# TensorE visits the attention once for two chunks from chunk 12 on; correction words in place; half of the down weights converted directly

## The chip, the cores and the metric

One core of one Trainium2 chip. The metric is the device time of one execution in microseconds (us). The kernel before was run three times.

## The reference, cut to what matters

Two stages. The first is a causal linear attention with a decay per head over (4, 8, 768, 64), in blocks of 64 tokens; the second takes its output as 3072 tokens of 512 values through a leaky ReLU layer pair. All inputs are 64-bit or 32-bit floats from the host's arrays; the weights (512x2048 and 2048x512) come as 64-bit floats.

```
for b in range(nb):
    intra = einsum('bhic,bhjc->bhij', qb, kb) * Dmask
    intra = einsum('bhij,bhjd->bhid', intra, vb)
    inter = einsum('bhid,bhde->bhie', qb * lam_pow, kv_state)
    out[:, :, sl] = intra + inter
    kv_state = lam_block * kv_state + einsum('bhsd,bhse->bhde', kb * rev_pow, vb)
x = out.transpose(0, 2, 1, 3).reshape(B * S, H * D)
h = x @ w_in
return maximum(0.01 * h, h) @ w_out
```

## The kernel before, in words

**Chunks and groups.** The 3072 tokens are 24 chunks of 128 (six to a batch), and four chunks make a group: six groups of 512 tokens. The attention works chunk by chunk, the layer pair group by group.

**Attention (L410, L546, L637 to L718).** For each chunk: load k, q and v; bring k and q into transposed form (on TensorE with `transpose`, L546, for chunks 0 to 9; for later ones by many small loads of 32x32 blocks, L509, and StreamTransposes on DVE, L518); scores into the PSUM tile psc (16 matmuls of 64x64) and state products k'v (16 matmuls, into the upper half of psc from chunk 4 on); on DVE the masking with the decay (L637, into the tile sc) and the state additions (L644); on POOL the decay of the state (L647), the scaling of k (L585) and of q (L592). The output of the chunk goes to the PSUM tile po: `own` (16 matmuls) and `inter` in two halves (8 and 8). The second half waits for a small read of po by DVE or ACT (L676). On TensorE a stay in the attention is: outputs of chunk c up to the first half of inter, then state products and scores of chunk c + 1, then the second half of inter of c: 64 matmuls, which the trace shows as two records each. These stays are called visits below.

**Splits.** A 32-bit value is carried to TensorE as three fp32r parts, high, low and mixed (h, l, m). Chunk outputs are split by ACT (L692, xh), DVE (L700, xl; L718, xm) into X of their group (two sets). The weights are split in `parts` (L807 or L809 wh, L812 wm, L814 wl) into W[p], p = 0 to 7, which the up weights fill first and the down weights later.

**64-bit weights.** `to_float32` (L764) makes 32-bit floats of a half row block: a load into one of the three buffers raw; on ACT, L793 (the upper words to w32), L795 and L797 (16-bit correction words, written to a dense buffer low0 or low1); on DVE a shift (L799) and the addition of the correction (L800).

**Up products (L850).** For each group g and weight block p: 2 halves x 3 parts x 4 = 24 matmuls of 512 columns into two of four PSUM banks (pt, b10, b11, b2); ACT applies the leaky ReLU (L877) into one of two tiles gs, and a DMA writes it to DRAM (L880). These and the down products are called wide matmuls below: 1152 and 1152.

**Down weights.** `w_out` converts one half of a row block at a time during groups 2 and 3 and writes it as 32-bit floats to DRAM (L829); in the last group `w_out_parts` (L831) reads a row block back and splits it into W[p] once the up product with W[p] is done.

**Down products (L916).** `down_load` (L888) reads a pair (g, p) back into one of four buffers over the attention's memory, splits it (L897 ACT, L898 and L900 DVE) into one of four ring slots, which lie over X; `down` accumulates pairs of p into eight PSUM accumulators.

**Order.** Every operation is entered into `Plan` with the tiles it reads and writes. The list ORDER (L266) gives operation numbers and engines in the order in which they stand in the program; what it doesn't name, `emit` places by the listed costs. Engines run their own operations in that order. SP issues all loads and stores but two. Negative entries of ORDER are fill matmuls on the identity (`busy`, L349) on TensorE.

Of the kernel before, what the change touches and what calls it, by code (L numbers as in the profile page):

```python
# [44 lines left out]
class Plan:  # L45
# [8 lines left out]
    def __init__(self, kinds, also, member):  # L54
        self.ops, self.rank = [], 0.0
        self.chain, self.chains = None, {}
        self.warm, self.slack, self.more = 0.0, 0.0, {}
        self.first = {"PE": 0.0, "ACT": 0.0, "DVE": 3.4, "POOL": 0.0, "DMA": 0.2}
        self.cold, self.idle, self.order = 4.75, None, []
        self.kinds, self.also, self.member = kinds, also, member  # L60
        self.deps, self.keys = None, None
# [24 lines left out]
    def resolve(self, program):  # L86

        last = {}
        ended = {x: -1 for names in self.kinds.values() for x in names}
        holds = dict.fromkeys(ended)  # L90
# [149 lines left out]
def kernel(  # L240
# [26 lines left out]
    APART = 4  # L267
    FIRST_LOADS = ["k0", "q0", "v0", "k1", "q1", "v1", "w10", "k2", "q2", "v2", "w11", "k3", "q3", "v3"]
    LOW_PE, MIX_PE = set(), set()
    PAIRS = {"q": set()}  # L270
    QS = 8
    KM = 8
    NRAW = 3
    TURN = 3
    SLACK, GSLACK = 4.0, 2.0
    EARLY_SLACK = 1.0
    GOFIRST = 3
    SUBL, FIRST = 0.75, -8.0

    DV = 10  # L280
    RUNS = {10: (-8.0, 0.8), 12: (4.0, 0.0)}
# [24 lines left out]
    raw = [sb([P, 2 * d_model], f"raw{i}") for i in range(NRAW)]  # L306
    lows = [sb([P, d_model], f"low{i}", I32) for i in range(2)]
    w32 = sb([P, 2, d_model], "w32")
    w32f = w32.rearrange("p h n -> p (h n)")
    tt = [raw[-1][:, i * T:(i + 1) * T] for i in range(2)]  # L310
    gs = [sb([P, 2, T], f"gs{i}") for i in range(2)]
    WO = [dram.tile([P, 2 * d_model], F32, name=f"wo{p}", tag=f"wo{p}") for p in range(NP)]
    G = [[dram.tile([P, 2 * T], F32, name=f"g{g}_{p}", tag=f"g{g}_{p}") for p in range(NP)] for g in range(NG)]


    NA = 9120
    att = sb([P, NA], "att")
# [24 lines left out]
    make_identity(nc, ident)  # L342

    def busy(n, at):

        wide = bank[at].rearrange("p (a t) -> p a t", t=C2)
        for i in range(0, n, 8):
            k = min(8, n - i)
            nc.tensor.matmul(wide[:, :k, :], lhsT=ident, rhs=_bc(ident[:, 0:C2], 1, k), start=True, stop=True, skip_group_check=True)  # L349

    busy(WARM, "b2")
    nc.gpsimd.memset(zero, 0.0)
    LATE_W = 5
    neg_i, pos_s = [W[LATE_W][2][:, i * P:(i + 1) * P] for i in range(2)]
    kinds = {"bank": list(bank), "raw": [f"raw{i}" for i in range(NRAW)], "low": ["low0", "low1"], "gs": ["gs0", "gs1"]}
    also = {"gs0": ["gs00", "gs01", "k@2", "v@2"], "gs1": ["gs10", "gs11", "k@3", "v@3"], f"raw{NRAW - 1}": [f"raw{NRAW - 1}", "q@3"], "psc": ["psc0", "psc1"], "po": ["po0", "po1"]}
    early = [Slot("gs", 0), Slot("gs", 1), Slot("raw", NRAW - 1)]
    plan = Plan(kinds, also, {"k@2": early[0], "v@2": early[0], "k@3": early[1], "v@3": early[1], "q@3": early[2]})
# [73 lines left out]
    def spot(nm, c):  # L432

        if (nm, c) in spots:
            return spots[nm, c].rearrange("p (h d) -> p h d", h=H), f"{nm}@{c}"
        return kqv["kqv".index(nm)][c % 2], f"{nm}{c % 2}"
# [33 lines left out]
    def run(c):  # L470

        lo = max(DV, c - c % TURN)
        return lo, c - c % TURN + TURN - lo
# [8 lines left out]
    def subs(first, n):  # L482


        n = n * C
        def rows(x, lo, hi):
            return x[:, :(hi - lo) * n].rearrange("p (y t) -> p y t", t=n), lo, hi
        ks = [(*rows(raw[-2], 0, 2), [hold(first, f"raw{NRAW - 2}")]), (*rows(raw[-1], 2, 4), [hold(first, f"raw{NRAW - 1}")])]
        qs = [(*rows(kqv_f[1], 0, HP), ["q0", "q1"])]

        if first == DV:
            ks = [(*rows(raw[0], 0, HP), [hold(first, "raw0")])]
        elif first < DV + TURN:
            qs = [(*rows(w32f, 0, 2), ["w320", "w321"])] + [
# [243 lines left out]
    def round_of(c):  # L738

        after = []  # L740
        if c + 2 < NCH:
            load_kq(c + 2)
# [8 lines left out]
        for x in after:  # L751
            x()
# [288 lines left out]
```

## Time and profile before

| | |
|---|---|
| three runs, us | 606.93, 608.06, 608.13 (median 608.06) |
| the profiled execution | 607.55 us, span 605.8 us, granted TensorE clock 0.999 |
| loads and stores | 105.18 MB in 147753 packets, 123632 of them under 512 bytes |
| DMA queue of SP | 59.2% of 16 engines' span |
| TensorE idle before its matmuls from 41 to 126 us | none; 0.48 us at 126.8 us |
| up products end, down products begin | about 341 us |

A trace row of TensorE is one record; PE is the matmul side, PEld the weight loads that run beside it. A group's mean lasts from its issue to its modelled end, so rows that overlap sum to more than the time they take; how far groups start from each other tells what they cost. DVE is VectorE, ACT ScalarE, POOL GpSimd, SP SyncE.

### The profile page before, as it was taken

The numbers are of one execution on the slowest core, as the hardware profiler recorded it, in microseconds if no ns is written. First come the engines' busy times: TensorE is split into PE (matmuls) and PEld (weight loads), VectorE is DVE, ScalarE is ACT, GpSimd is POOL, SyncE is SP. The second block draws the span as 40 slices with busy tenths as digits, with TensorE's granted clock in tenths as the row PEclk, the third lists the DMA queues.
The fourth block names the chain that finished last, engine by engine and source line by source line (L and its number), as shares of the span: only waits on it lengthen the run. The fifth ranks groups of instructions, "written<-read, shape, count | busy, mean of one in ns | idle before, by whom it ended". The sixth has DMA issues, their size and how long they took to land.

```text
span 605.8 us, 12704 instructions
## 1 busy us (share of the span) xinstructions
PE 597.7 (99%) x5376; PEld 494.6 (82%) x5376; DVE 296.5 (49%) x403; ACT 213.3 (35%) x329; POOL 79.2 (13%) x85
## 2 busy tenths in 40 slices
PE   8899999999999999999999999999999999999997
PEld 6788888878888888888888888888888888888886
DVE  6899865351453343244466764354353443534430
ACT  3677562212433343342555431222312313214111
POOL 2432532133132031033000000000000000000000
PEclk9999999999999999999999999999999999999999
DMA  9999877677888887774696842524333333333201
GB/s 208 246 255 270 222 194 193 124 190 186 236 198 219 233 234 202 192 227 160 204 349 245 291 160 84 160 85 139 124 109 135 111 132 122 123 104 123 86 1 69
DMA packets 147753, 105.18 MB, mean 174 GB/s; under 512 B 123632, under 2 KB 124400, under 8 KB 147696
## 3 DMA queue, kind: packets, MB, share of 16 engines
q1 hardware_dynamic: 147408, 104.29, 59.2%
q8 instruction: 42, 0.69, 0.5%
q14 instruction: 15, 0.12, 0.1%
q10 hardware_dynamic: 288, 0.07, 0.1%
HBM read 68.69 MB, written 35.65 MB: 172 GB/s over the span
## 4 chain that ended last, share of the span: by engine, by line
PE 96%; DVE 3%; issue 0%; POOL 0%; DVEq 0%; POOLq 0%
PE b L850 34%; PE b L916 16%; PE psc L916 11%; PE po L916 11%; PE pt L850 10%; PE pt L916 5%; PE po L410 4%; PE psc L410 3%; PE b L349 1%; PE po L546 0%; PE b L546 0%; DVE att L637 0%; DVE w L800 0%; PE pt L546 0%; DVE att L592 0%
## 5 line engine op out<-in xcount | busy, mean ns | idle before, releaser
L898 DVE SCALAR_TENSOR_TENSOR xl<-att,xh 128x1024 fp32r<-128x1024 f32 x48 | 58.7, 1223 | 126.4 <-ACT xh L897 126.4
L897 ACT ACTIVATE xh<-att 128x1024 fp32r<-128x1024 f32 x48 | 50.7, 1060 | 146.9 <-PE pt L916 69.9
L850 PE MATMUL b<-xl,wl 128*128 128x512 f32 (+1 forms) x304 | 79.9, 389 | 0.3 <-DVE wl L814 0.3
L850 PE MATMUL b<-xh,wh 128*128 128x512 f32 (+1 forms) x304 | 79.5, 391 | 0.0
L877 ACT ACTIVATE gs<-b 128x512 f32<-128x512 f32 x75 | 44.0, 596 | 98.9 <-PE b L850 77.0
L850 PE MATMUL b<-xm,wm 128*128 128x512 f32 (+1 forms) x304 | 78.3, 389 | 0.0
L850 PEld LDWEIGHTS b<-xl,wl 128*128 128x128 f32 x304 | 56.3, 188 | 12.4 <-DVE wl L814 0.4
L850 PEld LDWEIGHTS b<-xm,wm 128*128 128x128 f32 x304 | 56.2, 188 | 11.7
L850 PEld LDWEIGHTS b<-xh,wh 128*128 128x128 f32 x304 | 55.9, 188 | 11.6
L900 DVE SCALAR_TENSOR_TENSOR xm<-xl,xh 128x1024 fp32r<-128x1024 f32 x48 | 58.8, 1226 | 4.8
L916 PE MATMUL b<-wl,xl 128*128 128x512 f32 x144 | 56.0, 389 | 0.0
L916 PE MATMUL b<-wh,xh 128*128 128x512 f32 x144 | 56.0, 389 | 0.0
L916 PE MATMUL b<-wm,xm 128*128 128x512 f32 x144 | 56.0, 389 | 0.0
L647 POOL TENSOR_TENSOR att<-att 128x256 f32<-128x256 f32 x40 | 32.8, 819 | 106.4 <-DVE att L644 92.8
L916 PE MATMUL psc<-wm,xm 128*128 128x512 f32 (+1 forms) x100 | 38.2, 387 | 0.0
L916 PE MATMUL po<-wm,xm 128*128 128x512 f32 (+1 forms) x100 | 37.9, 384 | 0.0
L916 PE MATMUL po<-wh,xh 128*128 128x512 f32 x96 | 37.3, 389 | 0.0
L916 PE MATMUL psc<-wl,xl 128*128 128x512 f32 x96 | 37.3, 389 | 0.0
L916 PE MATMUL po<-wl,xl 128*128 128x512 f32 x96 | 37.3, 389 | 0.0
L916 PE MATMUL psc<-wh,xh 128*128 128x512 f32 x96 | 37.3, 389 | 0.0
L410 PEld LDWEIGHTS po<-att 64*64 64x64 f32 x1408 | 26.7, 134 | 8.1 <-issue 6.5
L410 PE MATMUL po<-att 64*64 64x64 f32 x1408 | 32.5, 222 | 0.5 <-DVE att L676 0.3
(105 smaller groups left out, 861.6 us busy)
## 6 DMA issues: line engine op xcount, KB each, us to landing
att<-g SPq DMA_DIRECT2D x48, 512.0 KB, 3.4
g<-gs SPq DMA_DIRECT2D x47, 512.0 KB, 3.6
raw<-in_moe_w_in_dram SPq DMA_DIRECT2D x16, 512.0 KB, 4.9
raw<-in_moe_w_out_dram SPq DMA_DIRECT2D x16, 512.0 KB, 4.4
out_dram<-gs SPq DMA_DIRECT2D x23, 256.0 KB, 2.2
att<-in_k_dram SPq DMA_DIRECT2D x44, 128.0 KB, 3.5
att<-in_v_dram SPq DMA_DIRECT2D x22, 256.0 KB, 4.2
wo<-w SPq DMA_DIRECT2D x8, 512.0 KB, 4.0
```

The lines of the kernel that those rows point to most:

```text
L349: nc.tensor.matmul(wide[:, :k, :], lhsT=ident, rhs=_bc(ident[:, 0:C2], 1, k), start=True, stop=True, skip_group_check=True)
L410: nc.tensor.matmul(dst[HALF[cols]], lhsT=lhsT[HALF[rows]], rhs=rhs[HALF[rows]], start=start, stop=True, skip_group_check=True)
L647: add("POOL", 0.62, lambda new=new, j=j: nc.gpsimd.tensor_tensor(state[(j + 1) % 4], new, _bc(lam_c, 2, D), op=ALU.mult), [f"st{j % 4}", " ...
L850: nc.tensor.matmul(dst, lhsT=w[z][:, kk * 2 * P + f * P:kk * 2 * P + (f + 1) * P], rhs=x[z][:, kk, toks], start=start and kk == 0, stop=kk ...
L877: add("ACT", ns, lambda b=b, r=r: nc.scalar.activation(out=r(), in_=b(), func=AF.Prelu, bias=0.0, scale=1.0, alpha=0.01), [kb], [kg], rank ...
L897: add("ACT", 1.05, lambda: nc.scalar.activation(out=h, in_=graw[j], func=AF.Copy, bias=0.0, scale=NEAR), reads, wr("h"))
L898: add("DVE", 1.215, lambda: nc.vector.scalar_tensor_tensor(l, graw[j], 1.0, h.bitcast(F32), op0=ALU.mult, op1=ALU.subtract), reads + [f"rh ...
L900: add("DVE", 1.215, lambda: nc.vector.scalar_tensor_tensor(m, l.bitcast(F32), -S, h.bitcast(F32), op0=ALU.mult, op1=ALU.add), [f"rh{j}", f ...
L916: nc.tensor.matmul(to[:, cols], lhsT=ring[j][z][:, f * T + tb * P:f * T + (tb + 1) * P], rhs=W[pp][z][:, f * d_model:(f + 1) * d_model][:, ...
```

## The change

Three edits, and a new ORDER list for all of it.

1. **Pairs.** From chunk 12 on the attention advances by two chunks. `pair_of(c)` enters `outputs([c, c + 1])`: own of both, first halves of inter of both, one small read of po, the scores and state products of c + 2 and c + 3, second halves of both. Odd chunks use the upper halves of psc and po, which state products and transposes had; state products of a pair go to two of the four banks of the up products, the even chunk in the lower half of both, the odd one in the upper. The masked scores of odd chunks (L665, two operations of 256 columns) lie in the ends of raw1 and raw2; v of every other pair in raw3; a fifth state buffer in the end of w32. The one visit behind chunk 11 already holds the scores of 12 and 13.
2. **Correction words in place.** The two buffers low go and a fourth raw comes. ACT writes the 16-bit correction words into the lower 32-bit word of each 64-bit one in raw (L870, L872), and DVE adds that word, every second one of raw, to w32 (L875). raw is held until that addition is done.
3. **Down weights.** p = 0 to 3 go through DRAM as before, a half at a time at a slower pace; p = 4 to 7 are loaded, converted and split in the last group (`w_out_direct`), without the way through DRAM.

The fill matmuls, loads and operations of the first 118 us stand in another order in the new list. The diff, cut:

```diff
-    NRAW = 3
+    NRAW = 4
-    DV = 10
+    DV, DW, M0 = 10, 12, 12
+    PHASE, SPREAD, NVIA = 2, 24, 4
-    lows = [sb([P, d_model], f"low{i}", I32) for i in range(2)]
+    state.append(w32f[:, 3 * HP * D:].rearrange("p (y d) -> p y d", y=HP))
+    sc_odd = [raw[1 + x][:, 3 * HP * D:].rearrange("p (y t) -> p y t", y=HP) for x in range(2)]
+    v_more = [raw[3][:, i * H * D:(i + 1) * H * D].rearrange("p (h d) -> p h d", h=H) for i in range(2)]
...
+    def banks_of(c):
+        return shared.setdefault(c // 2, [Slot("bank") for _ in range(2)])
...
-        apart = c < APART
-        kp = [Slot("bank") for _ in range(n_pu)] if apart else ["psc"] * n_pu
+        apart, odd = c < APART or c >= M0, c >= M0 and c % 2 == 1
+        kp = (banks_of(c) if c >= M0 else [Slot("bank") for _ in range(2)])[:n_pu] if apart else ["psc"] * n_pu
+        cols = slice(T // 2, T) if odd else slice(0, T // 2)
...
+            if odd:
+                for x in range(2):
+                    add("DVE", 0.42, lambda x=x: nc.vector.tensor_tensor(sc_odd[x], psc[:, x, upper, :], decay[:, x], op=ALU.mult), [psck, "fk"], [("sca", "scb")[x]])
...
+        for c, at, pok, needs, inter in todo:
+            add("PE", 0.235, lambda inter=inter: inter(0), needs + ["begun"], [pok], kind="q")
+        add(("DVE", "ACT"), (0.15, 0.25), lambda e: (nc.vector.tensor_copy if e == "DVE" else nc.scalar.copy)(seen_po, po[:, :, at.start, 0]),
+            [x[2] for x in todo], ["seen_po"], rank=-3.0)
         between()
+        for c, at, pok, needs, inter in todo:
+            add("PE", 0.235, lambda inter=inter: inter(1), needs + ["seen_po", "begun"], [pok], kind="q")
...
+    def pair_of(c):
+        after = []
+        plan.begin(c)
+        more = [x for x in (c + 2, c + 3) if x < NCH]
+        after.insert(0, outputs([c, c + 1], lambda: after.extend(scores(x) for x in more)))
+        plan.end()
+        for x in after:
+            x()
+        for x in more:
+            transposes(x)("s")
+        for x in (c + 4, c + 5):
+            if x < NCH:
+                follow(x)
...
         def addend(dt, i):
-            return low().bitcast(dt).rearrange("p (n two) -> p n two", two=2)[:, :, i]
+            return r().bitcast(dt).rearrange("p (n four) -> p n four", four=4)[:, :, i]
...
-        add("DVE", 0.69, lambda: nc.vector.tensor_tensor(d, d, low(), op=ALU.add), [kl], [key], lock=True)
+        add("DVE", 0.69, lambda: nc.vector.tensor_tensor(d, d, words(0, I32), op=ALU.add), [kr], [key], lock=True)
...
+        to_float32("wo", p, h, w32[:, 0, :], "w320", after)
+        move(0.8, lambda: nc.sync.dma_start(out=WO[p][:, h * d_model:(h + 1) * d_model], in_=w32[:, 0, :]), ["w320"], [f"WO{p}"])
+
+    def w_out_direct(p):
+        for h in range(2):
+            to_float32("wo", p, h, w32[:, h, :], f"w32{h}", (), h)
+        parts(p, w32f, ["w320", "w321"])
...
-        if nxt < NCH and nxt // GC < g + 2 and n % 2 == 0:
-            seq.append(("r", nxt))
-            nxt += 1
-        if n_out < 2 * NP and n >= 1:
+        if nxt < NCH and nxt // GC < g + 2 and n % 4 == PHASE:
+            seq.append(("p", nxt))
+            nxt += 2
+        if n_out < 2 * NVIA and n * 16 >= SPREAD * n_out + 16:
...
-            w_out_parts(x[1])
+            (w_out_parts if x[1] < NVIA else w_out_direct)(x[1])
```

More of the change, by code (lines that the diff above doesn't have):

```diff
@@ L487, in rows @@
             return x[:, :(hi - lo) * n].rearrange("p (y t) -> p y t", t=n), lo, hi
-        ks = [(*rows(raw[-2], 0, 2), [hold(first, f"raw{NRAW - 2}")]), (*rows(raw[-1], 2, 4), [hold(first, f"raw{NRAW - 1}")])]
+        ks = [(*rows(raw[1], 0, 2), ["kr1"]), (*rows(raw[2], 2, 4), ["kr2"])]
         qs = [(*rows(kqv_f[1], 0, HP), ["q0", "q1"])]
[L491 to L494, printed above, removed]
-                (*rows(lows[i].bitcast(F32), 2 + i, 3 + i), [hold(first, f"low{i}")]) for i in range(2)]
+        if first < DW:
+            ks = [(*rows(raw[3], 0, HP), [hold(first, "raw3")])]
+        elif first == DW:
+            qs = [(*rows(raw[0], 0, 2), [hold(first, "raw0")]), (*rows(w32f, 2, 4), ["w320", "w321"])]
         return ks, qs
@@ L630, in scores @@
         if c < GOFIRST:
-            add("PE", 0.47, go, [f"kT{i}", f"qT{i}"], ["psc"], kind="q")
+            add("PE", 0.47, go, [f"kT{i}", f"qT{i}"], [psck], kind="q")
         add("PE", 0.47, kv, [kk, kv_], kp, kind="q")
         if c >= GOFIRST:
-            add("PE", 0.47, go, [f"kT{i}", f"qT{i}"], ["psc"], kind="q")
+            add("PE", 0.47, go, [f"kT{i}", f"qT{i}"], [psck], kind="q")
         def uses():
-            add("DVE", 0.685, lambda: nc.vector.tensor_tensor(sc, psc[:, :, lower, :], decay, op=ALU.mult), ["psc", "fk"], ["sc"])
+            while waiting and not odd:
+                waiting.pop()()
@@ L638, in uses @@
+            if odd:
+                for x in range(2):
+                    add("DVE", 0.42, lambda x=x: nc.vector.tensor_tensor(sc_odd[x], psc[:, x, upper, :], decay[:, x], op=ALU.mult), [psck, "fk"], [("sca", "scb")[x]])
+            else:
+                add("DVE", 0.685, lambda: nc.vector.tensor_tensor(sc, psc[:, :, lower, :], decay, op=ALU.mult), [psck, "fk"], ["sc"])
             for t in range(n_pu):
                 j = 2 * c + t
-                new = state[j % 4]
+                at_j = turn_of(j)
+                new = state[at_j]
@@ L721, in outputs, with less @@
-        return uses
+        add("ACT", 0.595, lambda: nc.scalar.activation(out=tok(xh), in_=y, func=AF.Copy, bias=0.0, scale=NEAR), [pok], [h])
+        if c in LOW_PE:
+            def less():
+                for t in range(2):
+                    nc.tensor.matmul(y[:, t], lhsT=neg_i, rhs=tok(xh)[:, t], start=False, stop=True, skip_group_check=True)
+            add("PE", 0.26, less, [h, "neg_i", f"wm{LATE_W}"], [pok])
+            add(("ACT", "DVE"), (0.6, 0.685), lambda e: copy(e, tok(xl), y), [pok], [l])
+        else:
+            add("DVE", 0.685, lambda: nc.vector.tensor_tensor(tok(xl), y, tok(xh.bitcast(F32)), op=ALU.subtract),
+                [pok, h], [l])
@@ new lines, in split, with mix, negate @@
+        if c in MIX_PE:
+            mk = Slot("bank")
+            z = lambda: bank[mk.name].rearrange("p (k t) -> p k t", k=KO)
+            def mix():
+                nc.tensor.matmul(z(), lhsT=neg_i, rhs=xh, start=True, stop=False, skip_group_check=True)
+                nc.tensor.matmul(z(), lhsT=pos_s, rhs=xl, start=False, stop=True, skip_group_check=True)
+            add("PE", 0.46, mix, [h, l, "neg_i", "pos_s", f"wm{LATE_W}"], [mk])
+            def negate(e):
+                if e == "ACT":
+                    nc.scalar.activation(out=xm, in_=z(), func=AF.Copy, bias=0.0, scale=-1.0)
+                else:
+                    nc.vector.tensor_scalar(xm, z(), -1.0, None, op0=ALU.mult)
+            add(("ACT", "DVE"), (0.6, 0.685), negate, [mk], [m], rank=LATER if c < GC else 0.0)
+        else:
+            add("DVE", 0.69, lambda: nc.vector.scalar_tensor_tensor(xm, xl.bitcast(F32), -S, xh.bitcast(F32), op0=ALU.mult, op1=ALU.add),
+                [h, l], [m], rank=LATER if c < GC else 0.0, lock=True)
@@ L740, in round_of @@
         after = []
-        if c + 2 < NCH:
+        if c + 2 < NCH and c != M0 - 1:
             load_kq(c + 2)
@@ L1001 @@
                 add("DVE", 0.0, lambda: None, [], ATT + [f"gr{j}" for j in range(NR)])
-                add("ACT", 0.0, lambda: None, [], [f"raw{j}" for j in range(NRAW)] + ["t0", "t1"])
+                add("ACT", 0.0, lambda: None, [], ["raw0", "sca", "scb", "kr1", "kr2", "v2", "v3", "t0", "t1"])
+                add("DVE", 0.0, lambda: None, [], ["w320", "w321", "st4"])
                 freed = True
-            w_out_parts(x[1])
+            (w_out_parts if x[1] < NVIA else w_out_direct)(x[1])
         elif x[0] == "dl":
```

202 lines of the change are left out of this document (106 added, 96 removed), and 2 rows, old and new, of the table seq.

## The prediction

> **What bounds the kernel now.** First the page's busy shares, then the same by stretches (columns: microseconds; PE, PEld, DVE, ACT and POOL busy with their instructions; clock; DMA share; GB/s).
>
> ```profile
> PE 597.7 (99%) x5376; PEld 494.6 (82%) x5376; DVE 296.5 (49%) x403; ACT 213.3 (35%) x329; POOL 79.2 (13%) x85
> ```
>
> ```profile
> 9.00:29.00 20.00, 17.13 (x478) 14.23 (x470) 17.57 (x33) 12.87 (x22) 8.56 (x9) 1.00 1.00 247
> 29.00:57.00 28.00, 27.94 (x553) 24.20 (x553) 26.81 (x41) 20.61 (x37) 9.41 (x9) 1.00 1.01 263
> 57.00:118.00 61.00, 61.00 (x625) 50.23 (x624) 36.72 (x54) 28.15 (x49) 18.76 (x16) 1.00 0.74 188
> 118.00:295.00 177.00, 176.52 (x2292) 145.94 (x2291) 68.70 (x135) 62.40 (x114) 40.69 (x44) 1.00 0.75 207
> 295.00:341.00 46.00, 46.00 (x204) 38.04 (x203) 28.66 (x30) 23.32 (x35) 0.00 (x0) 1.00 0.78 279
> 341.00:606.00 265.00, 261.48 (x1157) 216.65 (x1155) 113.83 (x96) 63.52 (x72) 0.00 (x0) 1.00 0.35 114
> ```
>
> From 57 us on TensorE never starves; only TensorE's own time can be saved there. Before that, DVE is as full as TensorE (26.81 of 28 us), and between 9 and 29 us it is ahead of it: the chain of waits runs through DVE almost without a break from 12.8 to 26.9 us.
>
> What TensorE's time consists of, from the chain and from TensorE's timeline (start, length, group):
>
> ```profile
> 327.56 8.16 PE b L850 x36
> ```
>
> ```profile
> 163.19 0.93 PE L410 MATMUL po<-att 64*64 64x64 f32 x48
> 163.94 1.11 PE L410 MATMUL psc<-att 64*64 64x64 f32 x64
> 164.87 0.41 PE L410 MATMUL po<-att 64*64 64x64 f32 x16
> 165.21 1.19 PE L850 MATMUL b<-xm,wm 128*128 128x512 f32 x4
> 166.25 1.08 PE L850 MATMUL b<-xh,wh 128*128 128x512 f32 x4
> ```
>
> ```profile
> 292.21 0.93 PE L410 MATMUL po<-att 64*64 64x64 f32 x48
> 293.07 1.19 PE L850 MATMUL b<-xh,wh 128*128 128x512 f32 x4
> 294.20 0.46 PE L410 MATMUL po<-att 64*64 64x64 f32 x16
> ```
>
> A wide matmul takes 8.16 / 36 = 0.2267 us; the 2304 of them are 522.3 us of the 605.8 us span and don't change. A visit to the attention has 128 records and lasts from 163.19 to 165.21, 2.02 us. The wide runs between such visits last 0.23 us longer than their count times 0.2267 (0.13 at the head: 165.21 to 166.25 is 1.04 us for four that need 0.91; the rest at the tail). So a visit costs 2.25 us. The short one at 292.21 has 48 records and costs 0.86 + 0.22 = 1.08. Two equations: (2.25 - 1.08) / 80 = 14.6 ns a record, and **0.38 us for the visit itself**.
>
> **The change, part by part.** All sums start from the profiled execution, 607.55 us (span 605.8, 1.75 around it); the three runs have a median of 608.06.
>
> *Pairs.* I counted both instruction orders on TensorE: 1472 attention matmuls, 80 transposes and 2304 wide ones in each, so nothing is removed but visits. Behind the 308th wide matmul the order before has 15 visits, the new one 10 (one pair is cut in two, the last in two). 5 x 0.38 = **-1.9 us**. What could hide or undo it: the waits inside a visit. The second half of the state products waits for the small read of po (L676, 0.155 us), which the scores of two chunks (about 1.9 us) now cover instead of one. A pair's state products hold two of the four banks until four additions (0.41 each) and three decays on POOL (0.82 each) are done, some 5 us with their handovers; the up products then have two banks, 2.72 us each, against an eviction of 0.60. If ACT is late there, each pair loses up to 0.6 us (6 pairs: 3.6 us); I take 0, since 2.1 us cover it. xh, xl and xm of the second chunk come one split later (0.59 + 0.68 + 0.79 us); the nearest use is 24 wide matmuls (5.4 us) behind its visit.
>
> *Loads.* DVE and SP meet the pair at its first visit, behind wide matmul 340, which wants the transposed k and q of chunks 12 and 13; before, only chunk 12 was wanted, 8 wide matmuls earlier, and it was late:
>
> ```profile
> 127.26 1.16 PE L410 MATMUL psc<-att 64*64 64x64 f32 x64 [0.48 <-issue]
> ```
>
> Up to the last of the small loads of that run SP now issues 149 DMAs instead of 153 (0.47 us each), 1.9 us earlier, and the visit comes 8 wide matmuls (1.8 us) later. Against that stand four more StreamTransposes of 0.43. I leave the 0.5 us as it is: 0, with a bound of 2.6 us above (1.7 for the transposes and a landing of 2.8, less SP's 1.9).
>
> *The new written-out order in the first 57 us.* TensorE's fill matmuls (L349) sum to 5.63 rows of 512 columns before and 4.75 now; a row takes 0.893 us:
>
> ```profile
> L349 PE MATMUL b<-att 128*128 128x512 f32 x4 | 3.2, 893 | 1.4 <-POOL att L352 1.4
> ```
>
> They stand in for waits, so 0.88 x 0.89 = **-0.8 us**, if the waits are what the order supposes. On DVE, four operations that stood ahead of the second xm (L585 0.68, L637 0.68, L644 0.41, L700 0.68: 2.45 us) stand behind it now. Only L585 is gone (to POOL, 1.19); the rest is owed later, while DVE is still full, so I take no more than the 0.8.
>
> *Correction words in place.* ACT's three operations keep their count. The addition on DVE (L800) now reads every second 32-bit word of raw instead of a dense buffer. The rows:
>
> ```profile
> L800 DVE CUSTOM_DVE_ANT_0 w<-w,low 128x1024 uint16<-128x1024 uint16 x32 | 24.1, 764 | 6.4 <-ACT low L797 5.0
> L793 ACT ACTIVATE w<-raw 128x512 f32<-128x512 f32 x32 | 21.2, 667 | 6.9 <-DVE wm L812 3.5 <-DMA raw<-in_moe_w_in_dram 2.1 <-DMA raw<-in_moe_w_out_dram 1.3
> L898 DVE SCALAR_TENSOR_TENSOR xl<-att,xh 128x1024 fp32r<-128x1024 f32 x48 | 58.7, 1223 | 126.4 <-ACT xh L897 126.4
> ```
>
> No row shows DVE on such words. A gain is excluded: the same 512 additions. ACT reads just these words in 0.667 us where a dense 512 takes 0.59, +0.08; a DVE pass over as many words as the stride spans (L898) takes 0.46 more than L800. Between 0 and +0.46 I take +0.2, nearer to ACT's row, which reads the very same words. Ten of the 32 lie before 63.4 us, where the parts of the fifth weight are done and DVE is full: 2.0 us. Part of it lands in slack: wl of the last four of these weights is done 0.9 to 1.9 us before TensorE takes it (63.41 against 64.3 for the last), 1.2 us for the last two. So **+0.8 us** (0 to 3.4).
>
> [...]
>
> *Down weights.* Four of eight are no longer converted early, written out and read back; eight halves (ACT 0.667 + 0.788 + 0.782, DVE 0.574 + 0.764 each) move behind 295 us, where TensorE has no gap to give. Tightest is the mixed part (xm) of the sixth split of group 0, p = 5. Counted from the last up matmul: DVE does four ring splits (4.9 us), the rest of weight 6 (4.1) and a half of weight 7 (1.3), which fills the 48 wide matmuls (10.9 us) until ring slots come free; then ACT 1.06, splits and weight 7 on DVE 10.6: 22.6 us. It is wanted 104 wide matmuls on, at 23.6. Cost **0**; three strided additions at +0.2 still fit, at +0.46 it is 0.4 us late, once. The cover is thin.
>
> **Sum:** 607.55 - 1.9 - 0.8 + 0.8 = 605.65, and 0.1 for that thin cover: **605.8**.
>
> **Rivals.**
> 1. *The strided addition is dear.* For it: DVE is full until 65 us. Against: ACT's row. [...]
> 2. *Pair visits starve* (the slower side). Two chunks' k and q must have landed and be transposed at once, and a run's 32 small loads take SP 15 us. For it: the 0.48 us above, POOL and SP in order, the fill of DMA (0.75). Against: no such wait in the other visits, and the closest pairs (56 wide matmuls, 12.7 us) share a run. It decides once waits pass 1.8 us in all. One run of loads late by 5 us costs that once: 610.8.
> 3. *All of DVE's reordering arrives at TensorE*: 2.45 us instead of 0.8, and no price for the stride: 607.55 - 1.9 - 2.45 = 603.2. For it: the chain from 12.8 to 26.9 us is DVE. Against: DVE owes the work until 65 us.
> That the change doesn't do what it says is not open: the visits are counted in the order.
>
> **Numbers.** Forecast 0.45 (604.7 to 606.8), rival 3 0.17, rival 1 0.22, rival 2 0.16. About 0.2% (1.2 us) is what a measurement of this kernel can tell from no change. Forecast and rival 3 are faster (0.62), rival 1 the same (0.22), rival 2 slower (0.16). The range, 603.0 to 609.0, leaves out most of rival 2.
>
> **What would show it.** Visits of 256 records lasting 3.9 us with wide runs 0.23 over their count: the pairs are right; idle on TensorE inside them: rival 2. L875, the addition's new line, at 0.85 to 0.95 us: my price; over 1.1: rival 1. The 72nd wide matmul before 56.9 us: the new start is right. No gap on TensorE from 340 us on: the down weights are right. Wrong would make it a wait that I have not named in the first 57 us, where everything is full.

## The result, and the profile after

The changed kernel is slower: 616.35 us (median of four runs, 615.2 to 617.58) against 608.1 for the kernel before on the same chip, a ratio of 1.014 with a 95% interval of 1.011 to 1.017. The forecast was 605.8, its range 603.0 to 609.0.

From the page of the profile after, the busy shares, the instruction queue of part 3 (packets, MB, share of 16 engines) and the groups of the correction words:

```profile
PE 598.9 (98%) x5374; PEld 495.0 (81%) x5374; DVE 295.3 (48%) x405; ACT 245.8 (40%) x323; POOL 76.3 (12%) x86
...
q8 instruction: 42, 0.69, 0.5%
...
L872 ACT ACTIVATE raw<-raw 128x512 f16<-128x512 f32 x32 | 43.5, 1367 | 0.7
L870 ACT ACTIVATE raw<-raw 128x512 uint16<-128x512 uint32 x32 | 43.8, 1368 | 0.0
L875 DVE CUSTOM_DVE_ANT_0 w<-raw,w 128x1024 uint16<-128x1024 uint16 x32 | 23.7, 744 | 39.8 <-ACT raw L872 37.0
```

ACT is 32 us busier, through L870 and L872: 1.37 us each, 32 times, where L795 and L797 took 0.79 and 0.78 (37 us more). The addition, whose stride I had priced, costs 0.744 (0.764 before), but now waits 37 us for ACT.

The stretches of the prediction, after (microseconds; PE, PEld, DVE, ACT and POOL; clock; DMA share; GB/s):

```profile
29.00:57.00 28.00, 26.14 (x434) 21.88 (x435) 22.55 (x36) 25.14 (x36) 6.12 (x8) 1.00 0.96 238
57.00:118.00 61.00, 60.83 (x728) 49.88 (x727) 38.53 (x57) 37.44 (x50) 16.02 (x14) 1.00 0.76 199
118.00:295.00 177.00, 171.83 (x2245) 142.96 (x2244) 60.94 (x124) 57.56 (x89) 42.69 (x46) 1.00 0.67 178
295.00:341.00 46.00, 46.00 (x233) 38.03 (x232) 26.19 (x31) 30.24 (x40) 0.00 (x0) 1.00 0.78 277
341.00:606.00 265.00, 265.00 (x1170) 219.50 (x1169) 124.52 (x110) 75.16 (x84) 0.00 (x0) 1.00 0.35 116
```

From 29 to 57 us ACT is now the full engine (25.1 of 28 us; 20.6 before) and TensorE starves; from 118 to 295 us TensorE lacks 5.2 us, where before it lacked 0.5. Behind 295 us it lacks nothing. The grown span (605.8 to 613.4, 7.6 us) divides so:

| | before | after |
|---|---|---|
| until the visit at 111.37 us (before) and 113.17 us (after, 8 wide matmuls earlier in the order: 109.56 at equal count) | 109.56 | 113.17 (+3.6) |
| from there to the end of the last visit, less 0.2267 us for each wide matmul | 33.59 | 37.53 (+3.9) |
| from there to the end, less the same | 2.9 | 3.0 (0) |

**The first 3.6 us** lie on the chain of waits, which DVE carried from 12.8 to 26.9 us before (start, length, what; the largest shares from 8 to 60 us are now a load into raw with 17% and L870 and L872 with 15 and 11%):

```profile
24.11 1.27 ACT raw L870
...
25.41 1.37 ACT raw L872
...
29.41 5.30 DMA raw<-in_moe_w_in_dram
...
35.50 1.27 ACT raw L870
...
36.80 1.39 ACT raw L872
...
41.91 1.10 DVE w L875
```

Conversion after conversion runs through ACT, and the next load waits until ACT is through with raw.

**The other 3.9 us** are five stops. TensorE's timeline (start, length, group; in brackets the idle time before it and its releaser) at the visit that began at 164.44 us, and then the first matmul behind each of the other four stops:

```profile
167.27 0.23 PE L417 MATMUL po<-att,w 64*64 64x64 f32 x2
168.45 0.27 PE L417 MATMUL po<-att,w 64*64 64x64 f32 x2 [0.95 <-issue]
...
185.00 0.28 PE L417 MATMUL psc<-att 64*64 64x64 f32 x4 [0.24 <-issue]
217.83 0.21 PE L417 MATMUL b<-att 64*64 64x64 f32 x1 [0.86 <-issue]
244.80 0.50 PE L929 MATMUL b<-xl,wl 128*128 128x512 f32 x1 [1.72 <-issue]
280.02 0.21 PE L417 MATMUL psc<-att 64*64 64x64 f32 x1 [1.39 <-issue]
```

The stop at 167.3 us falls within one group of equal matmuls. "issue" says that the profile shows nothing that released it, and in the trace none of the five matmuls waits for a semaphore. (The wait of the kernel before at 127.26 us is marked "issue" too, but that matmul does wait for one.) From matmul start to matmul start the five lose 1.2, 0.4, 1.1, 1.9 and 1.6 us, 6.2 in all. Counted in records they stand 256, 380, 383 and 382 apart: multiples of 128 but for a few. A record is a weight load and a matmul, two instructions; with the 0, 7, 3 and 3 semaphore instructions that the trace has of TensorE between them they are 512, 767, 769 and 767 instructions apart, multiples of 256 to within one. The instruction queue moved 0.69 MB in 42 packets, 16 KB each, for TensorE's 10748 instructions of these records. The kernels of experiments 4 and 10, which add 2304 and 1792 instructions to TensorE, moved 51 and 49 packets: 9 and 7 more, or 256 instructions to a piece. What DMA moved just ahead of the first stop, from 166.2 to 167.3 us, is one such piece (it ran from 166.26 to 167.23):

```profile
DMA packets 1, 0.02 MB, mean 15 GB/s; under 512 B 0, under 2 KB 0, under 8 KB 0
...
q8 instruction: 1, 0.02, 5.5%
```

One more stop of this kind stands in the first stretch. It too falls within a group of equal matmuls that wait for no semaphore, it ends 1.5 us behind a 16 KB piece, and the kernel before has none like it from 8 us on:

```profile
16.16 0.69 PE L417 MATMUL po<-att 64*64 64x64 f32 x30 [1.12 <-issue]
```

So two theories for the test: **A**, ACT pays for 16-bit writes 8 bytes apart; **F**, TensorE's instructions come late where attention matmuls use up 128 records in 1.9 us. Their rivals are in the expectations.

### The profile page after: what moved, and what is told of

Read it like the earlier page. It is cut to its first block, busy times and chain, and to the rows that moved or that the text cites. A ratio compares the mean times of both kernels' runs of the same rounds, so it can differ in the third digit from the quotient of the medians.

```text
span 613.4 us, 12677 instructions
## 1 busy us (share of the span) xinstructions
PE 598.9 (98%) x5374; PEld 495.0 (81%) x5374; DVE 295.3 (48%) x405; ACT 245.8 (40%) x323; POOL 76.3 (12%) x86
## 4 chain that ended last, share of the span: by engine, by line
PE 92%; ACT 3%; DMA 1%; issue 1%; DVE 1%; SPq 1%; POOL 0%; DVEq 0%; POOLq 0%; ACTq 0%
PE b L929 31%; PE b L995 16%; PE psc L995 11%; PE po L995 11%; PE pt L929 10%; PE pt L995 5%; PE po L417 3%; PE psc L417 2%; DMA raw<-in_moe_w_in_dram 1%; ACT raw L870 1%; ACT raw L872 1%; PE b L417 1%; PE b L353 1%; PE b L554 0%; ACT w L868 0%
## 5 line engine op out<-in xcount | busy, mean ns | idle before, releaser
L929 PE MATMUL b<-xl,wl 128*128 128x512 f32 (+1 forms) x296 | 77.1, 386 | 2.2 <-issue 1.7
L929 PE MATMUL b<-xh,wh 128*128 128x512 f32 (+1 forms) x296 | 77.6, 388 | 0.1
L929 PE MATMUL b<-xm,wm 128*128 128x512 f32 (+1 forms) x296 | 75.6, 384 | 0.0
L929 PEld LDWEIGHTS b<-xl,wl 128*128 128x128 f32 x296 | 54.3, 188 | 14.3 <-issue 2.2
L929 PEld LDWEIGHTS b<-xm,wm 128*128 128x128 f32 x296 | 54.6, 188 | 11.1
L929 PEld LDWEIGHTS b<-xh,wh 128*128 128x128 f32 x296 | 54.0, 188 | 11.8 <-ACT att L535 0.3
L872 ACT ACTIVATE raw<-raw 128x512 f16<-128x512 f32 x32 | 43.5, 1367 | 0.7
L870 ACT ACTIVATE raw<-raw 128x512 uint16<-128x512 uint32 x32 | 43.8, 1368 | 0.0
L875 DVE CUSTOM_DVE_ANT_0 w<-raw,w 128x1024 uint16<-128x1024 uint16 x32 | 23.7, 744 | 39.8 <-ACT raw L872 37.0
```

The lines of the kernel that those rows point to most:

```text
L870: add("ACT", 0.78, lambda: nc.scalar.activation(out=addend(U16, 0), in_=words(0, U32), func=AF.Copy, bias=0.0, scale=2.0 ** -29), [], [kr])
L872: add("ACT", 0.78, lambda: nc.scalar.activation(out=addend(F16, 1), in_=words(1, F32), func=AF.Copy, bias=0.0, scale=2.0 ** -100), [], [kr])
L875: add("DVE", 0.69, lambda: nc.vector.tensor_tensor(d, d, words(0, I32), op=ALU.add), [kr], [key], lock=True)
L929: nc.tensor.matmul(dst, lhsT=w[z][:, kk * 2 * P + f * P:kk * 2 * P + (f + 1) * P], rhs=x[z][:, kk, toks], start=start and kk == 0, stop=kk ...
```

## The experiments

Ratios are to the kernel before on the same chip; a number in brackets behind one is its 95% interval. Starts and excesses come from one profiled execution each. "Start" is the time of the visit that came at 113.17 us in the changed kernel (109.56 before, at equal count), "excess" the second row of the table above.

### 1. The 8-byte step alone, in the kernel before

```diff
-    lows = [sb([P, d_model], f"low{i}", I32) for i in range(2)]
+    both = sb([P, 2 * d_model], "low", I32)
+    lows = [both.rearrange("p (n two) -> p n two", two=2)[:, :, i] for i in range(2)]
```

> The kernel before, with one thing changed: the two dense buffers for the 16-bit correction words become one of the same total size in which the words of one buffer stand between those of the other, so that ACT writes its 16-bit words 8 bytes apart (4 before) and DVE reads every second 32-bit word; nothing is written in place. Theory A (ACT's price is the 8-byte step of its 16-bit writes): the two ACT operations take 1.27 to 1.37 us instead of 0.788 and 0.782, the addition on DVE stays at 0.74 to 0.78, the 72nd wide matmul starts 2 to 4 us later than 56.95 us, and the time is 610 to 612.5 us. Rival B (the price comes from reading and writing the same buffer): the two operations stay at 0.78 and the time at 608 us. Rival C (the strided addition on DVE is dear, as in my first rival): the addition takes over 1.0 us.

Beside this one DVE operation stands one place later, and two early loads of q wait for both buffers instead of one.

Its groups by form:

```profile
L798 ACT ACTIVATE low<-raw 128x512 f16<-128x512 f32 x32 | 44.8, 1399 | 0.0
L796 ACT ACTIVATE low<-raw 128x512 uint16<-128x512 uint32 x32 | 43.9, 1384 | 2.6 <-DMA raw<-in_moe_w_in_dram 1.4 <-DMA raw<-in_moe_w_out_dram 0.6 <-DVE w L801 0.3
L801 DVE CUSTOM_DVE_ANT_0 w<-low,w 128x1024 uint16<-128x1024 uint16 x32 | 23.2, 736 | 11.6 <-ACT low L798 10.5
```

The price is the step's, not that of writing in place, and DVE pays nothing. But the time hardly moved: 608.85 us, ratio 1.001 (0.9995 to 1.003); the start came 1.1 us later, where 2 to 4 were expected for the 72nd wide matmul, and 0.7 us of that came back, since the wait of the kernel before at 127.26 us is gone. In the order of before most of ACT's 12 us on the ten early half blocks is covered. What it costs is decided by the order around it.

### 2. Dense words for the up weights, in the changed kernel

```diff
+    words5 = pool.tile([P, 2 * d_model], F32, name="words5", tag=f"wl{LATE_W}")
...
+        low = words5[:, n_raw % 2 * d_model:(n_raw % 2 + 1) * d_model] if kind == "wi" else None
-        add("DVE", 0.69, lambda: nc.vector.tensor_tensor(d, d, words(0, I32), op=ALU.add), [kr], [key], lock=True)
+        add("DVE", 0.69, lambda: nc.vector.tensor_tensor(d, d, correction(), op=ALU.add), [kr], [key], lock=True)
```

> The changed kernel, but for the eight up weights the correction words are written densely (4-byte step) into the memory that the low part of weight 5 takes later, and added from there; for the down weights they stay in place. The order of all operations stays. Theory A (of the 7.6 us that the span grew, 3.6 are ACT's dearer writes on the path of the first 60 us): ACT's two operations on the up weights take 0.78 us, the 72nd wide matmul starts before 57.5 us instead of at 59.83, the gaps of TensorE inside the pair visits stay as they are, and the time is 612 to 613.5 us. Rival (the start is late because of its new order of fills, loads and DVE operations, and ACT only waits less): the 72nd wide matmul stays behind 59 us and the time at 615 to 616.5 us.

```profile
L878 ACT ACTIVATE words<-raw 128x512 uint16<-128x512 uint32 x16 | 12.6, 785 | 0.0
L880 ACT ACTIVATE words<-raw 128x512 f16<-128x512 f32 x16 | 12.2, 769 | 0.0
L883 DVE CUSTOM_DVE_ANT_0 w<-raw,w 128x1024 uint16<-128x1024 uint16 x16 | 11.2, 702 | 25.5 <-ACT raw L880 25.1
L883 DVE CUSTOM_DVE_ANT_0 w<-w,words 128x1024 uint16<-128x1024 uint16 x16 | 11.1, 697 | 6.9 <-ACT words L880 6.3
```

612.79 us, ratio 1.007 (1.005 to 1.010): the start is back at 108.60 us and 3.6 us of the loss are gone. The start alone gives 4.6; the excess rose to 38.80, with the five stops at the same records. The last two rows are one operation with and without the stride, 0.702 and 0.697 us.

Later runs show how far single profiles differ. Up to this visit, 4, 7 and 10 have the order and the writes of the changed kernel, and their starts are 114.15, 113.42 and 113.32 us; 6, 8 and 9 have those of this one, with 109.79, 110.71 and 109.91. So a start varies by 1 to 2 us from profile to profile, and the two sets lie apart.

### 3. The same order of work, 64 records further on in the instruction stream

```diff
+    for i in range(32):
+        x, y = slice(i % 2 * D, (i % 2 + 1) * D), slice(i // 2 % 2 * D, (i // 2 % 2 + 1) * D)
+        nc.tensor.matmul(bank[("b10", "b11")[i % 2]][y, 0:D], lhsT=ident[x, 0:D], rhs=ident[x, 0:D], start=True, stop=True, skip_group_check=True)
```

> The changed kernel with 32 extra small matmuls (64 records, 0.9 us of work) on TensorE at the very start, while it waits for the first loads; their results are not used. Theory F (TensorE stands still at borders of its instruction stream, which is fetched in pieces of 16 KB, here 256 instructions or 128 records of a matmul and its weight load): everything behind stands 64 records further on in the stream, so each gap moves 64 records forward in its visit. The visit that started at 164.44 us had its gap behind record 189 of 240, the one at 182.33 behind 149 of 240, at 214.25 behind 169 of 256, at 275.38 behind 190 of 208, and the visit at 238.53 (208 records) behind the 4th wide matmul after it. With the shift the borders lie behind 125 and 253, 85 and 213, 105 and 233, 126 and 254, and 20 and 148: no gap in the first and the fourth of these, 0.4 to 1.2 us behind 213, 1.1 behind 233, 1.2 behind 148; the sum of the gaps falls from 6.2 to about 3.5 us and the time is 613.5 to 615.5 us. Rival W (the gaps are waits inside the visit for the read of po, for banks or for the transposed k and q): each gap stays at the same matmul with the same length, and the time is 616.3 to 617.3 us.

TensorE's timeline, the first matmul behind each stop in the visits that F named:

```profile
192.27 0.51 PE L420 MATMUL b<-raw,att 64*64 64x64 f32 x11 [1.39 <-issue]
225.86 0.28 PE L420 MATMUL po<-att 64*64 64x64 f32 x4 [1.75 <-issue]
248.76 0.33 PE L420 MATMUL psc<-att 64*64 64x64 f32 x4 [0.57 <-issue]
```

They stand behind records 211, 233 and 148 of their visits (213, 233 and 148 expected). The first and the fourth visit, which stopped behind 189 and 190, run through in 3.81 and 3.42 us. No wait on another engine would move so: W is out. The time did not follow (617.16 us; 613.5 to 615.5 expected, and 616.3 to 617.3 by W): the excess fell to 36.63, but the start came at 118.48 us, 5.3 us later instead of 0.9, and one new stop of 0.9 came at 139.9. The profile is of the longest of the four executions (619.63 us), and its granted clock fell in the first 57 us (columns as in the stretches above):

```profile
9.00:29.00 20.00, 16.11 (x444) 13.55 (x439) 15.65 (x27) 12.94 (x18) 8.17 (x8) 0.91 0.96 236
29.00:57.00 28.00, 25.73 (x487) 22.09 (x485) 20.25 (x34) 24.57 (x32) 5.41 (x7) 0.94 0.75 201
```

In the changed kernel the clock was 1.00 in both stretches. Here it was halved for two spells of 3.4 us, which can cost TensorE up to 3.4 us, an estimate from their length. A second stop of the same kind, of 1.0 us at 25.4, came as well. So this start doesn't show what the added matmuls cost.

### 4. Bursts of small matmuls, and ACT's forms by themselves

```diff
+        for i in range(BURSTS.get(n_up, 0) // 2):
+            r, c, y = i % 2, i // 2 % 2, i // 4 % HP
+            quad(psc[:, r, lower, :][:, y, :], r, l[:, 0:C2], x[:, 0:C2], c, start=True)
...
+        add("ACT", 1.3, lambda: nc.scalar.activation(out=to(), in_=w, func=AF.Copy, bias=0.0, scale=2.0 ** -29), [], ["raw0", "raw1"])
```

> The changed kernel with work added whose results are not used: behind the last visit, between wide matmuls, five bursts of small matmuls like those of the attention (64, 128, 192, 256 and 512 records) from weights that lie there into a free part of PSUM, with nothing to wait for; and in the down products, where ACT has slack, 32 ACT copies of the 512 lower words of a raw buffer in seven forms (16-bit words 4 bytes apart in another buffer; 8 bytes apart in another buffer; 8 bytes apart in place; 4 bytes apart in place; 32-bit words 8 bytes apart; 16-bit dense; 32-bit dense). Theory F (instruction pieces of 128 records, each only asked for about when the one ahead begins, with some 3.2 us from asking to use): 64 and 128 records last 0.93 and 1.9 us, 256 and 512 records stop at every border behind the first, 256 in about 5 us and 512 in 10 to 12 us. Rival W (the gaps are waits on other engines): every burst lasts its count times 14.6 ns, 3.8 and 7.5 us for the last two. For ACT, theory A: the 16-bit forms 8 bytes apart take about 1.3 us in place or not, those 4 bytes apart about 0.75 in place or not. Rival B: only the forms in place are dear.

ACT's forms, from the groups by form: in place 8 bytes apart, another buffer 8 bytes apart, in place 4 bytes apart, another buffer 4 bytes apart, and 32-bit words 8 bytes apart:

```profile
L997 ACT ACTIVATE raw<-raw 128x512 uint16<-128x512 uint32 x5 | 6.9, 1384 | 0.1
L994 ACT ACTIVATE raw<-raw 128x512 uint16<-128x512 uint32 x4 | 5.5, 1379 | 0.1
L1000 ACT ACTIVATE raw<-raw 128x512 uint16<-128x512 uint32 x5 | 3.9, 787 | 0.1
L991 ACT ACTIVATE raw<-raw 128x512 uint16<-128x512 uint32 x4 | 3.2, 797 | 0.1
L1003 ACT ACTIVATE raw<-raw 128x512 f32<-128x512 uint32 x5 | 3.4, 670 | 0.1
```

A to the number: 16-bit writes 8 bytes apart take 1.38 us in place or not, 4 bytes apart 0.79, and whole words at the same 8 bytes 0.67. The bursts, in TensorE's timeline:

```profile
301.38 1.16 PE L417 MATMUL psc<-wl,wh 64*64 64x64 f32 x64
309.04 2.10 PE L417 MATMUL psc<-wl,wh 64*64 64x64 f32 x128
...
330.25 3.25 PE L417 MATMUL psc<-wl,wh 64*64 64x64 f32 x206
336.95 0.97 PE L417 MATMUL psc<-wl,wh 64*64 64x64 f32 x50 [3.44 <-issue]
...
348.98 2.55 PE L417 MATMUL psc<-wl,wh 64*64 64x64 f32 x158
354.58 2.63 PE L417 MATMUL psc<-wl,wh 64*64 64x64 f32 x128 [3.05 <-issue]
```

With nothing to wait for, 64 and 128 records run through; 192 stop once, for 2.8 us; 256 last 7.6 us (with a stop of 3.4) and 512 last 14.8, more than the 5 and 10 to 12 expected. The pieces themselves began late here: that of the second-last burst at 334.69 us, 1.4 us behind the start of the stop. The last burst can't be held against its expectation, since the granted clock was halved in the middle of it:

```profile
348.98:363.80 14.82, 10.67 (x514) 10.27 (x513) 0.10 (x1) 1.04 (x1) 0.00 (x0) 0.77 0.22 83
355.90:362.70 6.80, 5.70 (x220) 5.51 (x212) 0.00 (x0) 0.00 (x0) 0.00 (x0) 0.50 0.01 2
```

### 5. The step back, raw freed early

```diff
-                return low.bitcast(dt).rearrange("p (n two) -> p n two", two=2)[:, :, i]
+                return words5.bitcast(dt).rearrange("p (n four) -> p n four", four=4)[:, :, 2 * at_low + i]
```

> As the kernel with dense words for the up weights (612.79 us, the 72nd wide matmul at 55.74 us and the visit behind the 308th at 117.20), but the words stand 8 bytes apart again, in the same memory of their own: two buffers, each word of one between two of the other. So ACT's two operations are as dear as in the changed kernel (1.37 us), while raw is given back as early as with dense words. Theory A (the dearer writes alone delay the start): the 72nd wide matmul starts at 59 to 60 us, the visit behind the 308th wide matmul at 121 to 122, the time is 615.5 to 617 us. Rival H (raw is held for longer, until the addition, so that loads come late): the start is as with dense words, 72nd at 56 to 57 us, the time 612.5 to 614 us. In between: both share it.

616.33 us, ratio 1.013 (1.011 to 1.016), start at 112.32: A. That raw is held longer costs nothing that shows in the time; the start is 0.9 to 1.8 us below the four with the words in place, little more than single profiles differ by.

### 6 and 7. The five visits cut in the middle

Eight wide matmuls that stood behind each visit go behind its first 128 records, with dense words (6) and in the changed kernel as it is (7):

```diff
 # ORDER, the visit of chunks 14 and 15 (numbers of TensorE's operations; 803 and 804 are wide)
 (721), (722), (727), (723), (724),
+(803), (804),
 (726), (728), (730), (731), (729), (830),
-(803), (804),
```

> The kernel with dense words for the up weights, and in each of the five visits of 208 to 256 records whose gaps I read as late instructions, 8 of the wide matmuls that followed stand in the middle, behind 128 records (two evictions stand earlier on ACT for it); nothing else changes. Theory F: 8 wide matmuls take 1.8 us and only 16 instructions, so the next 16 KB are there: the five gaps (1.1, 0.5, 1.2, 2.5 and 1.5 us, some 6.8) shrink to under 1.5 us in all, each cut costs 0.38 us (1.9), and the time is 607 to 609 us, as before the change. Rival W (waits on other engines inside the visits): a wait for the read of po or for banks is as well covered by 8 wide matmuls, so W too would take the gaps away, but its gaps did not move with the shift. Rival N (the gaps come from a full DMA and go on): they stay at over 4 us in all and the time is over 611 us.

> The changed kernel with the five visits cut in the middle in the same way, and the correction words in place as the change has them. Theory F with theory A: the two losses add up, so this one keeps the late start (72nd wide matmul at 59 to 60 us) and loses only the gaps: 6.2 us of gaps go, 1.9 us of visits come, 611.5 to 613 us. If the cuts gain more or less than with dense words, the two causes touch each other.

6 took 612.79 us, ratio 1.009 (1.007 to 1.010), 7 615.83, ratio 1.013 (1.011 to 1.015). The first halves last 2.02 us as in the kernel before, but almost nothing was won (607 to 609 and 611.5 to 613 us expected). TensorE's waits of 6 from 118 to 296 us (in total, times, longest):

```profile
PE b L942 <- DVE att L675: 1.8, 3, 1.1
PE pt L942 <- DVE att L675: 0.8, 1, 0.8
PE po L417 <- issue: 0.4, 1, 0.4
```

Where "issue" stood there is now, but for one stop of 0.4 us, DVE's state addition, for whose banks the wide matmuls wait. That is the price of held banks that the prediction had bounded at 0.6 us a pair and taken as 0; two of these waits (1.1 and 0.8) are longer than the bound. In the uncut visits no such wait shows.

### 8 and 9. The state chain

The additions wait for POOL's decays of the state (L678), which stand behind the scalings of q (L603, 1.0 to 1.3 us each). 8 puts the scalings behind the decays in three visits of the cut kernel, 9 in the uncut one with dense words:

```diff
 # ORDER, POOL's operations of one visit (749 and 750 scale q)
-(741), (750), (749), (743), (747)
+(741), (743), (747), (750), (749)
```

> Cutting the visits took the late instructions away but not the time (612.79 us with and without the cuts): in their place TensorE now waits 1.1, 0.6, 0.8 and 0.2 us behind the visits for banks that DVE's state additions still hold, and these wait for POOL's decays, behind one or two scalings of q (1.0 to 1.3 us each). This kernel is the cut one with POOL's scalings of q behind the decays in three of the visits (and the DVE transposes that overwrite that q behind them); TensorE's, ACT's and SP's orders are the same. Theory S (the state chain is the second limit, which the late instructions had hidden): the waits of TensorE for the additions behind the visits at 165, 184 and 216 us shrink from 1.7 us to under 0.5 in all, and the time is 610.5 to 612 us. Rival (the chain's length comes from its own four additions and three decays, not from what stands between): the waits stay and the time is 612.8.

> The kernel with dense words and uncut visits (612.79 us), with the same new order on POOL and DVE. By theory F the late instructions end after the state chain in these visits, so the chain is hidden behind them: gaps inside the visits as before (1.1 to 2.7 us), time 612.3 to 613.3 us. If instead the time falls by over 1 us, the state chain was the limit of the uncut visits too.

8 took 611.87 us, ratio 1.007 (1.005 to 1.010): behind these visits TensorE waited 1.7 us for the additions in 6 and doesn't now. TensorE's longest waits, same stretch:

```profile
PE pt L942 <- DVE att L675: 1.4, 1, 1.4
PE b L942 <- ACT gs L969: 0.6, 1, 0.6
```

What is left stands behind another visit, at 242.4 us (0.8 us in 6), and at 198.5 us for an eviction. The gain over 6 is inside the intervals. 9 took 612.14 us, ratio 1.008 (1.006 to 1.010), just under the 612.3 to 613.3 expected for uncut visits (612.79 without the new order), with its stops still "issue".

### 10. Bursts where DMA is quiet

```diff
+                n = {(2, 0): 128, (2, 2): 256, (4, 2): 512}.get((pps[0], tb), 0) if g == NG - 1 else 0
```

> The changed kernel with three bursts of small matmuls (128, 256 and 512 records, results not used, nothing to wait for) in the last group of the down products, where DMA is at 0.1 to 0.3 of its time instead of 0.75 as at the earlier bursts. Theory F1 (16 KB of instructions take about 3.2 to 3.5 us from asking to use by themselves): 512 records last 11 to 13 us (14.8 in the earlier burst), 256 records 5 to 6. Theory F2 (the delay is queueing behind data on the DMA engines): with DMA quiet a piece is there in under 2 us, and 256 and 512 records last close to 3.9 and 7.6 us.

The three bursts as stretches (length, then PE and its records, and so on as above):

```profile
580.09:582.12 2.03, 2.03 (x130) 1.96 (x129) 1.93 (x3) 0.72 (x1) 0.00 (x0) 1.00 0.00 0
587.79:593.00 5.21, 4.15 (x257) 3.94 (x257) 0.00 (x0) 0.00 (x0) 0.00 (x0) 1.00 0.01 3
604.13:616.85 12.72, 8.34 (x514) 7.86 (x513) 0.00 (x0) 0.00 (x0) 0.00 (x0) 1.00 0.02 5
```

With DMA at 0.02, 256 records last 5.2 and 512 last 12.7 us: F1. In the long burst the pieces began at 605.79, 609.32, 612.78 and 616.25 us, 3.5 us apart: 1.1 us from the end of a stop to the next piece, 0.9 to 1.0 for its 16 KB, 1.3 to 1.55 until TensorE went on. 128 records of work take 1.9 us, so a border costs 1.6. The burst of 256 took 2.4 us more in experiment 4, with DMA at 0.59 over its length; that DMA traffic is why is not shown. The bursts of 512 don't compare, because the clock differed.

### 11 and 12. Whole words in the first correction operation

```diff
-        add("ACT", 0.78, lambda: nc.scalar.activation(out=addend(U16, 0), in_=words(0, U32), ...
+        add("ACT", 0.78, lambda: nc.scalar.activation(out=whole(), in_=words(0, U32), ...
```

11 is the changed kernel, 12 that of experiment 9.

> The changed kernel, in which the first of ACT's two correction operations writes whole 32-bit words in place (its value in the lower half, zeros above) instead of 16-bit ones; the second then writes its 16 bits over the upper half as before. The bursts of ACT copies showed 32-bit words 8 bytes apart at 0.67 us and 16-bit ones at 1.38. Theory A: the first operation falls from 1.37 to about 0.67 us, the second stays at 1.37; 0.7 of the 1.17 us by which ACT's part of a half block grew is taken back, so the start comes back by about half to two thirds of 3.4 us and the time is 613.5 to 615 us; the gaps inside the visits stay. If the start does not move, ACT's time is not what holds it.

> The kernel with dense words for the up weights and POOL's scalings of q behind the decays (612.14 us), with the first correction operation writing whole 32-bit words: 0.67 us instead of 0.79 on the up weights and 0.67 instead of 1.37 on the down weights. Theory A: the words are then hardly on the path of the start any more (0.1 us a half block), 611.5 to 612.3 us; the gaps inside the visits keep this above the kernel before.

```profile
L875 ACT ACTIVATE raw<-raw 128x512 f16<-128x512 f32 x32 | 43.5, 1367 | 0.7
L873 ACT ACTIVATE raw<-raw 128x512 uint32<-128x512 uint32 x32 | 21.6, 674 | 0.0
```

11 took 614.27 us, ratio 1.010 (1.008 to 1.012), start at 111.22: 2 of the 3.6 us are back for half of ACT's price, though a start alone can differ by that much. 12 took 611.86 us, ratio 1.006 (1.004 to 1.008), the lowest median with pairs, which 8 and 9 match within their intervals, and slower than the kernel before.

## Why the prediction was wrong

- **Correction words in place (+0.8; it was +3.6).** The step that failed is "ACT's three operations keep their count". The count was right, but I carried their durations over although the edit changes where they write. I priced the read side on DVE, where there was nothing to pay, and not the write side on ACT: 2 x 0.58 us a half block. The rows I had could not have given it: all 16-bit writes before are 4 bytes apart. That is just where a bound from both sides was due and was not made. Rival 1 looked at the same edit and priced DVE too, at over 1.1 us an addition. No run shows such a price: in experiment 2 the addition took 0.702 us with the step of 8 bytes and 0.697 without.
- **Pairs (-1.9; it was +3.9).** The visit's fixed cost was right: cut visits last 2.02 us again, and the uncut one of 192 records 2.98 (192 x 0.0146 + 0.15 = 2.95). The step that failed is the look at "the waits inside a visit": I listed waits on engines and banks, and not TensorE's own instructions. By the later runs a visit with two borders of its stream inside or just behind it stops at the second, here for 0.4 to 1.9 us, and a visit of one chunk has at most one border. So pairing saves 0.38 us for each visit that goes and pays up to 1.9. 33.6 - 1.9 - 0.7 (the load wait of before, from matmul start to matmul start, which went) + 6.2 is 37.2, against 37.5 measured. What a border cost differed with how fast the records went. In the stretch of wide matmuls from 341 us on, where 128 records take 29 us (128 x 0.2267), no stop shows: TensorE is busy for 265.00 of 265 us. In the bursts of experiment 10, where they take 1.9 us, every border behind the first cost 1.3 to 1.9 us.
- **Banks held by a pair (0, with a bound of 3.6).** In the result 0; 2.6 us once the stops were gone (experiment 6), so the stops seem to have covered it.
- **Loads at the first pair visit (0, bound 2.6).** Right: the visit at 131.27 us has no gap, and the 0.5 us wait of before is gone. What was late there was not transposed k or q, as I had it, but by the trace most likely a load of v, which landed at 127.17 us, 0.1 ahead of the matmuls.
- **The new order in the first 57 us (-0.8).** Not shown. With dense words the start came at 108.60, 109.79, 110.71, 109.91 and 109.83 us in five kernels, against 109.56 before: between -1.0 and +1.2. The new order has ACT on its path: the same dearer writes cost 1.1 us in the order before and 2.5 to 4.6 in the new one (113.17 less these five). It also has the early instruction stop, of 0.2 to 1.8 us in every kernel of this order. Which of its moves puts ACT on the path isn't settled.
- **Down weights (0).** Right, though the slack at the sixth split was not measured: the 1388 wide records behind the last visit take 314.20 us, 0.2264 each, and the stretch from 341 us on has no gap.
- **The rivals.** Rival 2 had the slower side and named the pair visits, but for loads, which were in time. My sentence on what would make it wrong, a wait not named in the first 57 us, was half of it.

Open is how the 5.3 us of experiment 3 divide between clock, stop and added matmuls, and whether visits placed so that each sees one border only would earn the 1.9 us: it was not tried, since every change of the order moves the borders.

## What to carry to other kernels

When an edit changes an operand's layout, price every engine that touches it, the writer first, and bound the price if no row has that step and width. Work that is packed more densely on one engine must also be fed with instructions: count them, two for each record here (10748 for 5374), and ask how long the engine takes for 128 records and whether that is under the 3.5 us that a piece took here. A stop that is removed shows the next one behind it: the cuts and POOL's new order each took away the waits that they were meant to, and moved the time by 0 to 0.9 us.

## What the runs showed of the hardware

- In experiment 4 ACT took 1.38 us for 512 16-bit writes 8 bytes apart, 0.79 to 0.80 us 4 bytes apart, 0.675 us dense (L1006 of its groups), and 0.670 us for 32-bit writes 8 bytes apart. One buffer for source and target made no difference: 1.384 us in place against 1.379 apart, and 0.787 against 0.797.
- TensorE's instructions arrive in pieces of 16 KB: 42 packets, 0.69 MB in the changed kernel. In experiment 10, with DMA at 0.02, the pieces of a burst of 512 small records (14.6 ns each where nothing stops them) began 3.5 us apart, one for 128 records, and the burst lasted 12.7 us. In experiment 4 the bursts of 192 and 256 ran 170 and 206 records before they stopped, once each, for 2.8 and 3.4 us.
- In experiment 2 DVE's addition of 16-bit limbs took 0.697 us with a dense second source and 0.702 us with every second 32-bit word.
